# Attention feeding a gelu MLP on one core: a weight tile with its half index moved, and a new order of all steps

## The chip, the core and the metric

The kernel runs on one core of a Trainium2 chip. The metric is the device time of one execution in microseconds (us), lower is better. The engines are TensorE (PE, with its weight loads PEld), VectorE (DVE), ScalarE (ACT), GpSimd (POOL) and SyncE (SP), which issues the transfers.

## The reference, cut to what matters

Four batches of eight heads, 768 positions, 64 values a head; then an MLP from 512 to 2048 and back over the 3072 tokens.

```python
k_sum = k.reshape(B, H, nb, 32, D).max(axis=3)
v_sum = v.reshape(B, H, nb, 32, D).mean(axis=3)
scores_l = where(abs(i - j) < 16, scale * q @ k.T, -1e9)
scores_s = scale * q @ k_sum.T + log(32)
a = softmax(concatenate([scores_l, scores_s]))
x = (a @ concatenate([v, v_sum]))           # to (tokens, 512)
out = gelu(x @ w_in) @ w_out                # exact gelu
```

## The kernel before

All products run in 16-bit pairs: a value is a high part plus a low part, and a product of two values is three matmuls (high by high, high by low, low by high). The first six of 24 attention units use 32-bit matmuls instead.

**Attention.** Unit u is one batch, four heads and 256 query rows. Its steps are `scores` (PE, into the tile pss), `add_mask` or `evac` (out of pss to s), `maximum` (one all-partition reduction on POOL, line 858), `shift` (DVE, line 863) and `exponent` (ACT, line 866), the split into 16-bit parts `s_p_hi` (ACT) and `p_lo` (DVE), `sums` and `values` (PE, into psn and psv), then `norm_take`, `norm_cross`, `norm_rec`, `norm_spread`, `norm_mult` (DVE and ACT, which read psn and psv and free them), and `x_hi`, `x_lo`, the split of the result into the tile xos. The 32-bit units have `f_scores`, `f_sums` and `f_values` in place of the PE steps.

**First MLP product.** Chunk c is 256 tokens (units 2c and 2c+1). For chunks 0 to 3, `phase1 c i` multiplies the chunk by the i-th block of 256 columns of w_in. The remaining tokens are four groups b = 2 to 5 of two chunks; a group's product with w_in is done with seven block products in place of eight: `sp b q n` is product n of 1 to 7 for quarter q of the hidden columns, 12 matmuls each (line 1059). Products 1, 6, 7 and 4 of a quarter add up, one after the other, in one bank y; products 2 and 5 open the banks x and z, and 3 adds to z. Between them `snap b q n` (ACT, line 1070) copies the running sum y to SBUF after products 1, 6 and 7, `comb` (DVE, line 1077) adds such a copy to x or z, and `s_gelu`, `sg_hi`, `sg_lo` make the two parts of the second product's input in the tile gg. The banks y, x and z of all quarters share three places (the tag psh).

**Where the copies go.** The 16-bit w_in weights are in the tile ww: part z (high, low), row block k, column block i, and a half e of 128 columns within the block. Half e = 1 of the first two row blocks is read by no product once chunks 0 to 3 are done, and `snap` writes its copies there:

```python
z = (3 * q + n - 1) % 4
snaps[b, q, n] = ww[:, z // 2, z % 2, :, 1, :].bitcast(F32)
```

Product 1 reads half e = 0 of the same two row blocks as weights.

**Second MLP product.** `phase2 c i` is 12 matmuls of 128x512 (lines 1107 to 1109) into the tile pso; `store` (ACT, line 1114) and `put` (SP) carry it out. There is one pso bank, so the next one waits for `store`. Groups 4 and 5 use seven products here too (`so`, line 1295).

**Weights.** w_in and w_out come as 64-bit values; `wi_bits i 0..2` and `wo_bits` (DVE, lines 456, 461, 465) take the 32-bit value out of the raw bits, `wi_hi` (ACT) and `wi_lo` (DVE) split it into ww.

**What sets the order.** Everything is one list, ORDER, of 1778 steps. Each engine works through its instructions in the order of that list; waits between engines are placed by the framework wherever two instructions touch the same memory. A table SLOTS says which of a tag's buffers each tile takes. `fill` steps are matmuls on ones in the first 37 us, whose result nobody reads.

Of the kernel before, what the change touches and what calls it, by code (L numbers as in the profile page):

```python
# [88 lines left out]
fetch_k 1 3, f_sums 2, evac 3, load_q 4, norm_mult 1, s_k_hi 4, x_hi 1, norm_take 2, wi_hi 5, fill 10, k_lo 4, fetch_k
1 0, x_lo 1, f_mask 4, wi_bits 1 0, f_values 2, maximum 3, load_k 5, s_q_hi 4, load_v 3, load_vs 3, phase1 0 4, wi_lo  # L90
5, shift 3, exponent 3, norm_cross 2, wi_hi 3, wi_bits 1 1, q_lo 4, load_v 4, wi_bits 1 2, fetch_w_in 6 2, phase1 0 0,
gelu 0 0, norm_rec 2, load_vs 4, phase1 0 5, norm_spread 2, f_sums 3, wi_lo 3, norm_mult 2, prep_k 1 3, wi_hi 1,
s_k_hi 5, norm_take 3, k_lo 5, scores 4, f_values 3, gelu 0 4, x_hi 2, wi_lo 1, phase1 0 3, phase1 0 1, norm_cross 3,
x_lo 2, load_q 5, wi_bits 6 0, wi_hi 2, evac 4, norm_rec 3, wi_lo 2, gelu 0 5, norm_spread 3, fetch_w_in 7 3, phase1 0
2, g_hi 0 5, g_hi 0 0, s_q_hi 5, prep_k 1 0, fetch_w_out 0 4, norm_mult 3, g_lo 0 0, x_hi 3, gelu 0 1, gelu 0 3, g_lo
0 5, maximum 4, x_lo 3, gelu 0 2, phase1 1 5, phase1 1 4, shift 4, g_hi 0 1, q_lo 5, wi_bits 7 0, g_hi 0 4, fetch_k 1
1, wo_bits 0 0, exponent 4, g_hi 0 2, fetch_w_out 1 5, g_lo 0 1, g_hi 0 3, wi_bits 6 1, wo_bits 0 1, g_lo 0 3, wo_bits
0 2, load_mask, wo_hi 0, g_lo 0 4, wi_bits 6 2, f_sums 4, f_values 4, f_mask 5, scores 5, phase1 1 2, wi_bits 7 1,
# [5 lines left out]
6, fetch_w_out 4 4, wo_bits 3 1, norm_spread 4, wo_hi 2, phase1 1 6, s_k_hi 6, g_lo 0 2, gelu 1 0, phase1 1 7, wo_bits
3 2, fetch_w_out 5 5, shift 5, exponent 5, k_sums 1 0, k_lo 6, wo_hi 3, norm_mult 4, g_hi 1 0, load_q 7, phase2 0 1,
wo_lo 2, wo_bits 4 0, wo_lo 3, x_hi 4, wo_bits 4 1, f_sums 5, wo_bits 5 0, g_hi 0 6, load_vs 5, wo_bits 4 2, f_mask 6,
wo_bits 5 1, norm_take 5, load_k 7, wo_bits 5 2, scores 6, phase2 0 2, s_q_hi 7, f_values 5, evac 6, fetch_w_out 6 4,
wo_hi 4, wo_lo 4, g_hi 0 7, wo_hi 5, wo_lo 5, norm_cross 5, norm_rec 5, norm_spread 5, fetch_v 1 2, x_lo 4, f_mask 7,
# [5 lines left out]
7, wo_bits 7 2, fetch_v 1 0, wo_lo 6, fetch_v 1 3, sums 6, wo_hi 7, s_k_hi 9, fetch_v 2 1, phase1 2 7, wo_lo 7,
norm_take 6, phase2 0 6, prep_v 1 0, k_lo 9, phase2 0 7, store 0 0, fetch_k 2 3, prep_v 1 3, evac 7, maximum 7, prep_v
2 1, phase2 1 0, phase2 1 2, phase2 1 4, norm_cross 6, g_hi 2 6, prep_k 2 3, load_k 8, wt_add 1 0, s_q_hi 9, shift 7,
q_lo 9, g_hi 2 1, g_lo 2 1, load_vs 6, v_hi 6, g_lo 2 0, gelu 2 3, load_vs 7, wt_add 1 1, v_lo 6, s_k_hi 8, fetch_v 2
2, put 0 0, load_q 8, fetch_k 2 0, k_lo 8, load_k 11, g_lo 2 4, gelu 2 7, phase2 1 6, g_lo 2 6, norm_rec 6, values 6,
v_hi 7, load_v 8, exponent 7, v_lo 7, norm_spread 6, scores 9, phase1 2 2, prep_k 2 0, load_v 9, g_hi 2 3, s_q_hi 8,
s_k_hi 11, wt_add 1 2, s_p_hi 7, q_lo 8, add_mask 9, phase1 2 5, store 1 0, load_q 11, k_lo 11, p_lo 7, norm_mult 6,  # L120
maximum 9, x_hi 6, values 7, sums 7, load_vs 8, prep_v 2 2, x_lo 6, s_q_hi 11, wt_hi 1, q_lo 11, scores 8, g_hi 2 7,
wt_lo 1, norm_take 7, load_vs 9, shift 9, norm_cross 7, norm_rec 7, phase2 1 1, phase2 1 3, phase2 1 5, load_q 10,
add_mask 8, put 1 0, maximum 8, load_k 10, gelu 2 2, norm_spread 7, norm_mult 7, v_hi 9, x_hi 7, x_lo 7, v_hi 8, store
# [1326 lines left out]
```

## Time and profile before

| | |
|---|---|
| median of 3 runs | 569.73 us (568.25 to 572.7) |
| the profiled execution | 572.59 us, of which the span from first to last instruction is 570.8 us |
| TensorE busy | 556.9 us, 98% of the span |
| VectorE busy | 477.3 us, 84% |
| ScalarE busy | 382.0 us, 67% |
| GpSimd busy | 90.4 us, 16% |
| mean granted TensorE clock | 0.991 of full speed |

The profiled execution is 2.9 us above the median of the three runs. Busy shares of PE count a matmul from its start to its modelled end, and matmuls overlap, so a busy PE may still have short gaps between starts; a row with idle time before it is a true wait.

### The profile page before, as it was taken

The page shows a single profiled execution, that of the slowest core. Times are in us where ns is not written, and L with a number is a line of the kernel's source. Part 1 is how long each engine was busy: PE and PEld are TensorE (multiplying, and loading weights), DVE is VectorE, ACT ScalarE, POOL GpSimd, SP SyncE. Part 2 cuts the span into 40 slices and gives each one's busy share as a digit, 9 for nine tenths or more (in the row PEclk, how much of TensorE's full clock was granted, in tenths as well). Part 3 has the DMA queues.
Part 4 walks back from the last instruction along what each step waited for, and adds up shares of the span by engine and source line. Part 5 has one row for each costly group of instructions (what it writes and reads, how often), then busy time and mean ns, then how long its engine had stood idle before and what let it go on. Part 6 is the DMA issues. An engine that isn't in the chain of part 4 may idle for free.

```text
span 570.8 us, 13982 instructions
## 1 busy us (share of the span) xinstructions
PE 556.9 (98%) x6011; PEld 404.4 (71%) x6011; DVE 477.3 (84%) x660; ACT 382.0 (67%) x663; POOL 90.4 (16%) x42
## 2 busy tenths in 40 slices
PE   8969999999999999999979999999999999999997
PEld 4548887584766766667745677766567788888886
DVE  5999999999989899987995777788689999638831
ACT  3758775866696996878962769887547565545621
POOL 3532221202222250031222030203000000000000
PEclk9999999999999999999979999999999999999999
DMA  8969465656644433345251313220000000000101
GB/s 328 396 239 335 154 258 189 206 160 188 199 123 120 140 98 96 84 135 154 74 162 61 87 46 96 76 64 20 20 20 1 20 1 1 11 1 1 65 10 65
DMA packets 29230, 64.30 MB, mean 113 GB/s; under 512 B 2800, under 2 KB 8688, under 8 KB 29168
## 3 DMA queue, kind: packets, MB, share of 16 engines
q1 hardware_dynamic: 29168, 63.41, 33.8%
q8 instruction: 47, 0.77, 0.5%
...
HBM read 55.34 MB, written 6.29 MB: 108 GB/s over the span
## 4 chain that ended last, share of the span: by engine, by line
PE 79%; DVE 14%; ACT 3%; DMA 1%; issue 1%; POOL 1%; SPq 0%; DVEq 0%; POOLq 0%
PE psy L1059 14%; PE pso L1107 9%; PE pso L1109 9%; PE pso L1108 9%; PE psz L1059 7%; PE psd_y L1295 4%; PE psx L1059 4%; PE pso_y L1295 3%; PE psh L988 3%; PE pss_x L1295 3%; PE psh L989 3%; PE psh L990 3%; PE psv L911 3%; PE pss L829 3%; PE psv_z L1295 2%; DVE wt L465 2%
## 5 line engine op out<-in xcount | busy, mean ns | idle before, releaser
L858 POOL PARTITION_ALL_REDUCE m<-s x23 | 79.9, 3472 | 295.7 <-DVE s L849 94.7
L1107 PE MATMUL pso<-w_out_h,gg 128*128 128x512 f16 x256 | 97.2, 380 | 0.0
L1108 PE MATMUL pso<-w_out_l,gg 128*128 128x512 f16 x256 | 97.1, 379 | 0.0
L1109 PE MATMUL pso<-w_out_h,gg 128*128 128x512 f16 x256 | 97.1, 379 | 0.0
L1059 PEld LDWEIGHTS <-wt 128*128 128x128 f16 x768 | 74.9, 98 | 11.9 <-issue 0.4
L988 PE MATMUL psh<-xos,ww 128*128 128x256 f16 x256 | 70.3, 275 | 0.1
L989 PE MATMUL psh<-xos,ww 128*128 128x256 f16 x256 | 70.2, 274 | 0.2 <-DVE xos L968 0.2
L990 PE MATMUL psh<-xos,ww 128*128 128x256 f16 x256 | 70.1, 274 | 0.0
L1059 PE MATMUL psy<-xos,wt 128*128 128x256 f16 x576 | 70.0, 273 | 0.0
L1059 PEld LDWEIGHTS <-ww 128*128 128x128 f16 x576 | 56.4, 99 | 13.7 <-ACT ww L1070 3.7
L1109 PEld LDWEIGHTS <-gg 128*128 128x128 f16 x256 | 25.0, 98 | 30.4 <-issue 0.3
L1107 PEld LDWEIGHTS <-gg 128*128 128x128 f16 x256 | 25.0, 98 | 26.4
L1108 PEld LDWEIGHTS <-gg 128*128 128x128 f16 x256 | 25.1, 98 | 26.1
L1295 PEld LDWEIGHTS <-gg 128*128 128x128 f16 x384 | 37.5, 98 | 4.7 <-DVE gg L1187 0.3
L1070 ACT ACTIVATE ww<-psy 128x512 f32<-128x512 f32 x48 | 28.0, 589 | 16.2 <-PE psy L1059 15.3
L1091 DVE SCALAR_TENSOR_TENSOR gg<-g,gg 128x512 f16<-128x512 f32 x32 | 24.1, 764 | 8.7 <-ACT gg L1087 8.5
L863 DVE TENSOR_TENSOR s<-s,m 128x1024 f32<-128x1024 f32 x21 | 25.5, 1214 | 3.4 <-POOL m L858 3.4
L988 PEld LDWEIGHTS <-ww 128*128 128x128 f16 x256 | 25.1, 98 | 4.0 <-issue 0.2
L1059 PE MATMUL psy<-xos,ww 128*128 128x256 f16 x192 | 24.8, 282 | 3.2 <-ACT ww L1070 3.2
L1187 DVE SCALAR_TENSOR_TENSOR gg<-h,gg 128x512 f16<-128x512 f32 x32 | 21.6, 685 | 7.5 <-ACT gg L1184 7.3
L989 PEld LDWEIGHTS <-ww 128*128 128x128 f16 x256 | 25.2, 98 | 3.7 <-issue 0.3
L990 PEld LDWEIGHTS <-ww 128*128 128x128 f16 x256 | 25.2, 98 | 3.4 <-issue 0.4
...
## 6 DMA issues: line engine op xcount, KB each, us to landing
...
```

The source lines that it names most:

```text
L858: nc.gpsimd.partition_all_reduce(out_ap=self.m32, in_ap=self.s32, channels=P, reduce_op=bass_isa.ReduceOp.max)
L863: nc.vector.tensor_tensor(out=self.s32, in0=self.s32, in1=self.m32, op=ALU.subtract)
L988: nc.tensor.matmul(ph[:, e, :], wh, xh, start=(k == 0), stop=False)
L989: nc.tensor.matmul(ph[:, e, :], wh, xl, start=False, stop=False)
L990: nc.tensor.matmul(ph[:, e, :], wl, xh, start=False, stop=(k == NCC - 1))
L1059: nc.tensor.matmul(ps[:, e, :], ws, xx, start=(first and e == 0 and k == 0 and m == 0), stop=(k == 1 and m == 2), skip_group_check=True,)
L1070: nc.scalar.activation(snaps[b, q, n], split8(acc[b, q, "y"]), AF.Copy)
L1091: nc.vector.scalar_tensor_tensor(out=g_part(o // 2, q, 1, fs), in0=g32t.pop((b, q, o)), scalar=SC_G, in1=g_part(o // 2, q, 0, fs), op0=ALU ...
L1107: nc.tensor.matmul(p, gh, w_out_h[:, f, :], start=(f == 0), stop=False)
L1108: nc.tensor.matmul(p, gh, w_out_l[:, f, :], start=False, stop=False)
L1109: nc.tensor.matmul(p, gl, w_out_h[:, f, :], start=False, stop=(f == NFC - 1))
L1295: nc.tensor.matmul(ps, g, ww_, start=(first and e == 0 and k == 0), stop=(e == 1 and k == 2), skip_group_check=True,)
```

## The change

The tile ww gets its half index e ahead of the column block i, so that each half of a row block is one contiguous piece; all lines that read or write ww follow. The steps of ORDER are the same 1778, none added or left out, in a new order, and SLOTS is new to fit. Of both tables only a line is shown.

```diff
 ORDER = '''
-fill 1, load_q 0, fetch_k 0 0, load_m16, f_mask 0, prep_k 0 0, k_pack 0, f_scores 0, prep_k_end 0 0, fetch_w_in 0 0,
+load_q 0, fill 1, fetch_k 0 0, prep_k 0 0, load_m16, prep_k_end 0 0, k_pack 0, fetch_w_in 0 0, k_sums 0 0, load_ind,
...
     "ks16": (
-        "01101010"
+        "01010101"
     ),
...
-    ww = const.tile([P, 2, NCC, NFC // 2, 2, P], F16, name="ww")
+    ww = const.tile([P, 2, NCC, 2, NFC // 2, P], F16, name="ww")
...
     def w_part(i, z, ks=slice(0, NCC)):
-        return ww[:, z, ks, i].rearrange("p k e j -> p k (e j)")
+        return ww[:, z, ks, :, i].rearrange("p k e j -> p (k e) j")
...
     def wi_rows(i):
-        return wt[:, i].rearrange("p (k n) -> p k n", k=NCC)
+        return wt[:, i].rearrange("p (r j) -> p r j", j=P)
...
-                wh, wl = (ww[:, z, k, i, e, :] for z in range(2))
+                wh, wl = (ww[:, z, k, e, i, :] for z in range(2))
...
-                    wh, wl = (ww[:, z, 2 * w[0] + k, i, w[1], :] for z in range(2))
+                    wh, wl = (ww[:, z, 2 * w[0] + k, w[1], i, :] for z in range(2))
...
     def snap(b, q, n):
         z = (3 * q + n - 1) % 4
-        snaps[b, q, n] = ww[:, z // 2, z % 2, :, 1, :].bitcast(F32)
+        snaps[b, q, n] = ww[:, z // 2, z % 2, 1].bitcast(F32)
```

ORDER is two lines longer, so every line number behind it is two higher in the changed kernel.

The first place is TensorE in the middle of the kernel, where before the last matmuls of `phase2 4 6` (pso_4_0) are followed by `sp 3 1 1` (psy_3_1), on PE before:

```order
L1108 LDWEIGHTS gg_92
L1108 MATMUL pso_4_0_4201<-w_out_l_91,gg_92 128x512
L1109 LDWEIGHTS gg_92
L1109 MATMUL pso_4_0_4201<-w_out_h_90,gg_92 128x512
L1059 LDWEIGHTS ww_86 [waits Activation_49]
L1059 MATMUL psy_3_1_4471<-xos_89,ww_86 128x256 [waits PE_49]
```

In the change `scores 18`, `sums 16`, `values 16`, `phase2 5 0` and `sp 3 1 2` (psx_3_1) stand between the two, and the weight load of `sp 3 1 1` has no wait; on PE now, the last matmuls of `sp 3 1 2` and the first of `sp 3 1 1`:

```order
L1061 LDWEIGHTS ww_86
L1061 MATMUL psx_3_1_4640<-xos_89,ww_86 128x256
...
L1061 LDWEIGHTS ww_86
L1061 MATMUL psy_3_1_4653<-xos_89,ww_86 128x256 [waits DVE_49]
L1061 LDWEIGHTS ww_86
L1061 MATMUL psy_3_1_4653<-xos_89,ww_86 128x256
```

The wait on ScalarE is gone from the weight load; the matmul behind it waits for a VectorE step, the one that frees its bank.

ScalarE at the same place before, from `store 4 0` (ot_4_0) by `s_q_hi 20`, `s_gelu 2 3 2` and two `sg_hi` to `snap 3 0 1` (ww<-psy_3_0):

```order
L1114 ACTIVATE ot_4_0_4456<-pso_4_0_4201 128x512 [waits DMAHW0_49,PE_49]
L794 ACTIVATE qh_20_4458<-q32_20_4298 128x512 [waits DMAHW1_49]
L1084 ACTIVATE g32_2_3_2_4461<-psy_2_3_3944 128x512 [waits DVE_49]
L1087 ACTIVATE gg_92<-g32_2_2_3_4153 128x2x256
L1087 ACTIVATE gg_92<-g32_2_3_2_4461 128x2x256 [waits Activation_49]
L1070 ACTIVATE ww_86<-psy_3_0_4395 128x8x64
```

And ScalarE now:

```order
L1086 ACTIVATE g32_2_2_2_4532<-psy_2_2_3667 128x512 [waits DVE_49]
L1089 ACTIVATE gg_92<-g32_2_2_2_4532 128x2x256 [waits Activation_49]
L1116 ACTIVATE ot_4_0_4536<-pso_4_0_4135 128x512 [waits DMAHW4_49,PE_49]
L1029 ACTIVATE xos_89<-x32s_88 128x512 [waits DVE_49]
L1072 ACTIVATE ww_86<-psy_3_0_4399 128x512
```

Three instructions fewer stand between `store 4 0` and `snap 3 0 1`.

The second place is ScalarE some 10 us earlier, around `snap 2 3 3` (ww<-psy_2_3), which PE needs before `sp 2 3 4`, and `s_gelu 2 3 2` (g32<-psy_2_3), which frees the bank that `sp 3 0 1` takes in the change. Before:

```order
L965 ACTIVATE xos_89<-x32s_88 128x512
L1070 ACTIVATE ww_86<-psy_2_3_3944 128x8x64 [waits PE_49]
L1087 ACTIVATE gg_92<-g32_2_2_1_4232 128x2x256 [waits Activation_49]
L602 ACTIVATE k_all_93<-ks16_3_0_4352 128x2x4x24 [waits DVE_49] x2
L942 ACTIVATE rc_15_4389<-dent_15_4241 128x16
```

And now, with `exponent 16` (s32_16) and its table load ahead, `s_k_hi 18` (k_all), `norm_cross 15` (rc_15) and a table load in between:

```order
L868 ACT_TABLE_LOAD
L868 ACTIVATE s32_16_4181<-s32_16_4181 128x1024 [waits DVE_49]
L1072 ACTIVATE ww_86<-psy_2_3_3945 128x512 [waits PE_49]
L1089 ACTIVATE gg_92<-g32_2_2_1_4184 128x2x256 [waits Activation_49]
L739 ACTIVATE k_all_93<-k32_18_4029 128x10x64 [waits DMAHW1_49]
L944 ACTIVATE rc_15_4370<-dent_15_4361 128x16 [waits DVE_49]
L949 ACTIVATE rc_15_4370<-dent_15_4361 32x8 [waits Activation_49]
L949 ACTIVATE rc_15_4370<-dent_15_4361 32x8 x3
L1086 ACT_TABLE_LOAD [waits DVE_49]
L1086 ACTIVATE g32_2_3_2_4377<-psy_2_3_3945 128x512 [waits PE_49]
```

`exponent 16` moved ahead of `snap 2 3 3`; `s_gelu 2 3 2` moved up from behind `store 4 0`. Over the whole kernel ScalarE has 36 table loads in place of 34.

VectorE at the same place, from `add_mask 16` (s32_16<-pss_16) to `shift 16`, on which `exponent 16` waits, before:

```order
L849 SCALAR_TENSOR_TENSOR s32_16_4230<-mask_sb_79,pss_16_3977 128x1024
L1077 TENSOR_TENSOR g32_2_2_1_4232<-psz_2_2_4128,ww_86 128x512 [waits DVE_49,PE_49]
L934 STREAM_TRANSPOSE dent_15_4241<-psn_15_4219 128x256 [waits PE_49]
L589 TENSOR_REDUCE ks32_3_4228<-kp_3_0_4167 128x24 [waits DMAHW5_49]
L803 TENSOR_TENSOR ql_18_4296<-q32_18_4120,qh_18_4169 128x512 [waits DMAHW2_49]
L597 CAST ks16_3_0_4352<-ks32_3_4228 128x48 [waits DVE_49]
L598 TENSOR_TENSOR ks16_3_0_4352<-ks32_3_4228,ks16_3_0_4352 128x48 [waits DVE_49]
L1091 SCALAR_TENSOR_TENSOR gg_92<-g32_2_2_2_4118,gg_92 128x2x256
L1091 SCALAR_TENSOR_TENSOR gg_92<-g32_2_2_1_4232,gg_92 128x2x256 [waits Activation_49]
L863 TENSOR_TENSOR s32_16_4230<-s32_16_4230,m32_16_4244 128x1024 [waits Pool_49]
```

And VectorE now:

```order
L851 SCALAR_TENSOR_TENSOR s32_16_4181<-mask_sb_79,pss_16_3977 128x1024
L963 TENSOR_TENSOR x32s_88<-psv_14_4033,dent_14_4094 128x512 [waits DVE_49]
L1079 TENSOR_TENSOR g32_2_2_1_4184<-psz_2_2_4099,ww_86 128x512 [waits PE_49]
L640 TENSOR_REDUCE vs_3_3646<-vb_3_2_3908 96x32 [waits DMAHW6_49]
L1093 SCALAR_TENSOR_TENSOR gg_92<-g32_2_2_0_3897,gg_92 128x2x256 [waits Activation_49]
L970 TENSOR_TENSOR xos_89<-x32s_88,xos_89 128x512
L865 TENSOR_TENSOR s32_16_4181<-s32_16_4181,m32_16_4312 128x1024 [waits Pool_49]
```

`norm_take 15` (dent_15), `q_lo 18` (ql_18) and two `sg_lo` (gg) stand behind `shift 16` now; `norm_mult 14` and an `x_lo` (xos) stand between the two steps.

The third place is VectorE near the start, from `norm_mult 0` (x32s<-psv_0) to `norm_mult 1` (x32s<-psv_1), before:

```order
L961 TENSOR_TENSOR x32s_88<-psv_0_316,dent_0_285 128x512 [waits PE_49]
L465 SCALAR_TENSOR_TENSOR wt_87<-gg_92,wt_87 128x1024 [waits DVE_49]
L968 TENSOR_TENSOR xos_89<-x32s_88,xos_89 128x512 [waits Activation_49]
L934 STREAM_TRANSPOSE dent_1_390<-psn_1_348 128x256 [waits PE_49]
L456 TENSOR_SCALAR wt_87<-gg_92 128x1024 [waits DMAHW1_49]
L461 SCALAR_TENSOR_TENSOR wt_87<-gg_92,wt_87 128x1024 [waits DVE_49]
L950 RECIPROCAL rc_1_393<-rc_1_393 128x16 [waits Activation_49]
L954 STREAM_TRANSPOSE dent_1_390<-rc_1_393 128x512 [waits DVE_49]
L465 SCALAR_TENSOR_TENSOR wt_87<-gg_92,wt_87 128x1024
L961 TENSOR_TENSOR x32s_88<-psv_1_363,dent_1_390 128x512 [waits DVE_49,PE_49]
```

And now:

```order
L963 TENSOR_TENSOR x32s_88<-psv_0_314,dent_0_282 128x512 [waits PE_49]
L467 SCALAR_TENSOR_TENSOR wt_87<-gg_92,wt_87 128x1024 [waits DVE_49]
L936 STREAM_TRANSPOSE dent_1_368<-psn_1_356 128x256 [waits DVE_49,PE_49]
L970 TENSOR_TENSOR xos_89<-x32s_88,xos_89 128x512 [waits Activation_49]
L458 TENSOR_SCALAR wt_87<-gg_92 128x1024 [waits DMAHW1_49]
L463 SCALAR_TENSOR_TENSOR wt_87<-gg_92,wt_87 128x1024 [waits DVE_49]
L952 RECIPROCAL rc_1_395<-rc_1_395 128x16 [waits Activation_49]
L956 STREAM_TRANSPOSE dent_1_368<-rc_1_395 128x512 [waits DVE_49]
L467 SCALAR_TENSOR_TENSOR wt_87<-gg_92,wt_87 128x1024
L963 TENSOR_TENSOR x32s_88<-psv_1_372,dent_1_368 128x512 [waits DVE_49,PE_49]
```

`norm_take 1` (the transpose of psn_1) moved ahead of `x_lo 0`; the rest stands as it did. TensorE's own steps up to `f_values 2` stand in the same order in both.

## Rows read from the trace of the kernel before

**Rows 1.** The page, part 1: busy time, share of the span, instructions.

```profile
PE 556.9 (98%) x6011; PEld 404.4 (71%) x6011; DVE 477.3 (84%) x660; ACT 382.0 (67%) x663; POOL 90.4 (16%) x42
```

**Rows 2.** Windows: length, busy time (instructions) of each engine, granted clock, DMA.

```profile
40.00:60.00 20.00, 18.76 (x245) 16.16 (x246) 19.53 (x28) 15.37 (x29) 7.25 (x4) 0.91 0.82 290
60.00:280.00 220.00, 219.61 (x2632) 153.82 (x2630) 208.16 (x278) 171.08 (x281) 41.89 (x14) 1.00 0.47 147
280.00:300.00 20.00, 16.78 (x160) 10.50 (x160) 19.74 (x28) 14.53 (x28) 4.39 (x2) 0.85 0.47 148
...
294.90:297.60 2.70, 2.70 (x16) 1.67 (x20) 2.63 (x6) 0.40 (x1) 0.00 (x0) 0.50 0.95 282
297.60:300.40 2.80, 2.80 (x92) 2.33 (x94) 2.80 (x5) 2.78 (x5) 0.00 (x0) 0.50 0.31 101
```

**Rows 3.** Waits of PE: who for whom, total, times, longest.

```profile
PE psy L1059 <- ACT ww L1070: 3.2, 1, 3.2
PE psv L775 <- POOL m L858: 3.2, 1, 3.2
```

**Rows 4.** The chain that ended last, 276 to 301 us: start, us, what.

```profile
285.13 1.31 PE psz L1059 x12
...
291.66 0.60 ACT ot L1114
...
294.84 2.74 PE psy L1059 x12
```

**Rows 5.** Timeline of DVE, 276 to 292 us: start, us, instruction.

```profile
278.31 0.44 DVE L934 STREAM_TRANSPOSE dent<-psn 128x256 f32<-128x256 f32 x1
...
279.50 0.88 DVE L803 TENSOR_TENSOR ql<-q,qh 128x512 f16<-128x512 f32 x1
...
281.37 1.29 DVE L1091 SCALAR_TENSOR_TENSOR gg<-g,gg 128x512 f16<-128x512 f32 x2
282.57 1.22 DVE L863 TENSOR_TENSOR s<-s,m 128x1024 f32<-128x1024 f32 x1
...
286.57 0.68 DVE L1077 TENSOR_TENSOR g<-psz,ww 128x512 f32<-128x512 f32 x1
```

**Rows 6.** Timelines of DVE, PE, ACT and POOL in turn, 33 to 41 us.

```profile
33.29 1.52 DVE L968 TENSOR_TENSOR xos<-x32s,xos 128x512 f16<-128x512 f32 x1
34.73 0.44 DVE L934 STREAM_TRANSPOSE dent<-psn 128x256 f32<-128x256 f32 x1
...
37.84 2.70 DVE L465 SCALAR_TENSOR_TENSOR wt<-gg,wt 128x1024 int32<-128x1024 int32 x1
40.46 0.68 DVE L961 TENSOR_TENSOR x32s<-psv,dent 128x512 f32<-128x512 f32 x1
...
35.07 0.19 PE L829 MATMUL pss<-qh,k_all 64*128 64x64 f16 x2
...
36.38 1.02 ACT L845 ACTIVATE s<-pss 128x1024 f32<-128x1024 f32 x1
...
37.57 3.22 POOL L858 PARTITION_ALL_REDUCE m<-s  x1 [3.30 <-ACT s L845]
```

**Rows 7.** Groups of DVE by form: busy us, mean ns.

```profile
L465 DVE SCALAR_TENSOR_TENSOR wst<-x32s,wst 128x1024 int32<-128x1024 int32 x4 | 4.8, 1209 | 0.0
```

**Rows 8.** Timeline of ACT, 276 to 291 us.

```profile
278.42 0.63 ACT L1084 ACTIVATE g<-g 128x512 f32<-128x512 f32 x1
...
279.48 0.58 ACT L1070 ACTIVATE ww<-psy 128x512 f32<-128x512 f32 x1
...
281.76 0.21 ACT L942 ACTIVATE rc<-dent 128x16 f32<-128x16 f32 x1
282.01 0.89 ACT L947 ACTIVATE rc<-dent 32x8 f32<-32x8 f32 x4
282.91 1.28 ACT L866 ACT_TABLE_LOAD   x1
284.20 1.06 ACT L866 ACTIVATE s<-s 128x1024 f32<-128x1024 f32 x1
```

More of the change, by code (lines that the diff above doesn't have):

```diff
@@ L89 @@
[L89 to L98, printed above, removed]
@@ L104 @@
[L104 to L108, printed above, removed]
@@ L114 @@
[L114 to L123, printed above, removed]
@@ new lines @@
+2 0 1, s_gelu 2 1 1, sg_hi 2 1 1, maximum 14, sg_lo 2 0 1, sp 2 2 2, shift 15, comb 2 2 0, shift 14, norm_cross 13,
+s_q_hi 16, fetch_v 3 2, q_lo 16, exponent 14, sg_hi 2 1 2, s_p_hi 14, sp 2 3 2, phase2 3 7, norm_rec 13, load_q 18,
+exponent 15, sp 2 3 1, snap 2 3 1, sg_lo 2 1 3, norm_spread 13, k_lo 16, sg_lo 2 1 1, fetch_k 3 0, sp 2 2 7, scores
+16, p_lo 14, norm_mult 13, load_k 18, comb 2 3 0, values 14, sums 14, store 3 1, sg_lo 2 1 2, norm_take 14, s_p_hi 15,
+x_hi 12, sp 2 2 5, norm_cross 14, prep_k 3 0, snap 2 2 3, prep_k_end 3 0, sp 2 3 6, phase2 4 0, snap 2 3 2, p_lo 15,
@@ new lines @@
+x_hi 13, s_gelu 2 2 0, comb 2 2 3, sp 2 2 3, norm_rec 14, norm_spread 14, sp 2 2 4, add_mask 16, norm_mult 14, comb 2
+2 1, s_gelu 2 2 3, sp 2 3 5, values 15, s_gelu 2 3 0, scores 17, sg_hi 2 2 0, sums 15, load_v 16, sg_hi 2 3 0, maximum
+16, sp 2 3 7, prep_v 3 2, phase2 4 2, sg_lo 2 2 0, s_gelu 2 2 1, fetch_k 3 2, x_lo 13, put 3 1, shift 16, exponent 16,
+snap 2 3 3, sg_hi 2 2 1, sp 2 3 4, norm_take 15, sg_lo 2 3 0, fetch_k 3 3, comb 2 3 3, prep_k 3 2, s_k_hi 18,
+norm_cross 15, x_lo 12, s_gelu 2 3 2, sp 2 3 3, sg_hi 2 2 3, s_p_hi 16, sg_lo 2 2 1, s_gelu 2 3 3, load_vs 16, k_lo
@@ new lines @@
+3 1 7, norm_mult 16, phase2 4 1, s_k_hi 20, q_lo 19, scores 19, add_mask 19, s_gelu 3 0 0, s_gelu 3 0 2, values 17,
+v_lo 18, sums 17, norm_take 17, norm_cross 17, norm_rec 17, put 5 0, maximum 19, sp 3 0 3, phase2 4 3, phase2 4 5,
+s_gelu 3 0 3, sg_hi 3 0 0, sg_lo 3 0 0, k_lo 20, shift 19, load_k 21, phase2 4 7, norm_spread 17, s_p_hi 18, comb 3 0
+1, s_gelu 3 0 1, sg_hi 3 0 1, exponent 19, sp 3 2 1, p_lo 18, sp 3 1 5, s_k_hi 21, snap 3 2 1, snap 3 1 3, store 4 1,
+sums 18, norm_mult 17, load_q 21, values 18, s_q_hi 21, scores 20, k_lo 21, norm_take 18, sp 3 2 6, phase2 5 1,
@@ new lines @@
+shift 20, load_vs 20, v_hi 20, values 19, comb 3 2 3, sums 19, sp 3 2 4, s_q_hi 22, q_lo 22, sg_lo 3 0 2, x_hi 16,
+norm_take 19, sp 3 2 3, comb 3 2 1, add_mask 21, snap 3 3 1, sp 3 3 6, norm_cross 19, phase2 5 5, maximum 21, sg_hi 3
+1 2, snap 3 3 2, s_gelu 3 2 1, sg_lo 3 1 2, phase2 5 7, exponent 20, s_gelu 3 2 2, sp 3 3 7, put 4 1, norm_rec 19, sp
+3 3 2, norm_spread 19, sg_lo 3 2 0, shift 21, v_lo 20, sg_hi 3 2 2, load_k 23, sp 3 3 5, store 5 1, s_p_hi 20,
+norm_mult 19, sg_lo 3 2 2, snap 3 3 3, sp 3 3 4, comb 3 3 0, load_vs 22, x_hi 19, phase2 6 0, comb 3 3 3, s_gelu 3 3
```

319 lines of the change are left out of this document (163 added, 156 removed).

## The prediction

> **What bounds the kernel now.** The page's first part comes first: TensorE is busy 98% of the span, VectorE 84%, ScalarE 67% [rows 1]. A reader should see that nothing is left to gain but TensorE's few pauses, and that VectorE is the only other engine near its limit. The windows say where the pauses are: from 60 to 280 us TensorE is busy 219.61 us of 220 at a granted clock of 1.00, with VectorE busy 208.16 of the 220; from 40 to 60 us and from 280 to 300 us the clock is 0.91 and 0.85 [rows 2]. The waits of TensorE then give two of 3.2 us each and no other of that size: `sp 3 1 1` (psy, L1059) for ScalarE's write into ww (`snap`), and `f_values 2` (psv, L775) for a line on GpSimd [rows 3]. Both happen just before or in the windows with the low clock.
>
> The chain of waits shows the first closely. `phase2 4 6` ends and releases `store 4 0` on ScalarE at 291.66; the chain goes on through ScalarE's queue, and `sp 3 1 1` starts at 294.84 [rows 4]. Its 12 matmuls take 2.74 us, while 12 of the same shape took 1.31 us at 285.13 [rows 4]. From 294.9 to 300.4 us the granted clock is 0.50, the 1.2 GHz level [rows 2]: 2.70 and 2.80 us, 5.5 us in all, at half speed. The full level, 2.4 GHz, was granted in the 220 us ahead, in which TensorE had hardly paused; it fell after the pause.
>
> Is that wait a true one? What `sp 3 1 1` writes to, a bank that `comb 2 3 1` was the last to read, was free at 286.57 + 0.68 = 287.25 [rows 5], long before 291.6. What it waits for is `snap 3 0 1`, which writes half e = 1 of ww, while `sp 3 1 1` reads half e = 0. The bytes differ; only the interleaved pieces overlap.
>
> **The change part by part.** The sum is made against the profiled execution, 572.59 us (span 570.8, 1.8 around it). The steps are the same, so TensorE's own work stays, and each term is a pause or a stretch of low clock.
>
> *The wait at 291.6.* With e ahead of i the two halves are separate pieces, and in the new order the weight load of `sp 3 1 1` has no wait for ScalarE. The 3.2 us go [rows 3], and with them the stretch at 0.50: 5.5 us at half speed do the work of 2.75, so 2.75 are lost. 3.2 + 2.75 = 6.0 us. The lower bound is 3.2, if the clock falls there for another reason; the upper one 6.0. I take −6.0, since the clock was 1.00 for the 220 us without a pause. What is late next is `comb 3 0 0`, which the matmul of `sp 3 1 1` now waits for on VectorE. ScalarE's `snap 3 0 1` has three instructions fewer ahead of it, so `comb` can start earlier than it could.
>
> *The start.* `f_values 2` waits for `norm_mult 1` (starts 40.46), behind `wi_bits 3 2` (37.84, 2.70 us) [rows 6]. The same operation on 128x1024 elsewhere takes 1.21 us [rows 7]; this one ran beside GpSimd's `maximum 3` (37.57 to 40.79), which started when `evac 3` (L845, 36.38) was done [rows 6]. The first 34 VectorE instructions are the same set in another order, so their sum gains nothing by itself. But `norm_take 1` (0.44 us at 34.73) no longer stands behind `x_lo 0` (1.52 us at 33.29) [rows 6], which lets `norm_cross 1` on ScalarE and `evac 3` behind it go earlier. `evac 3` needs pss, whose last matmul ended at 35.07 + 0.19 = 35.26; so it can be 36.38 − 35.26 = 1.1 us earlier, GpSimd ends 1.1 earlier, and VectorE is let go 1.1 earlier. The bounds are 0, and 5.0 if the wait goes with its clock: 3.2 and 0.09 x 20 = 1.8 [rows 2, 3]. I take −1.1, the value that a chain of rows gives.
>
> Here the trace can be held against a rule. VectorE's instruction with two SBUF inputs took 2.70 us beside GpSimd's reduction, and 1.21 us elsewhere. The Trainium skill, page "SBUF — State Buffer", section "Who interferes with whom", says that such an instruction and a GpSimd instruction that reads SBUF exclude each other, and whichever issues second waits until the first ends. The trace agrees in that `wi_bits 3 2` ended at 40.54, 0.25 us ahead of `maximum 3`'s end. By the rule an earlier `maximum 3` would first wait for the two-input instruction ahead of `wi_bits 3 2`; an estimate from the page is that some half of the gain goes, and the sum would be half a microsecond higher.
>
> *New tight places in the middle.* Before `sp 3 0 1` the changed order needs a bank freed by `s_gelu 2 3 2`, and ScalarE has ahead of that `exponent 16`, `snap 2 3 3`, an `sg_hi`, `s_k_hi 18`, `norm_cross 15` and a table load. From the start of `snap`, by the rows: 0.58 (the snap), 0.63 (`sg_hi`, priced as the `s_gelu` of the same size), 0.79 (`s_k_hi`, an estimate of mine: 640 columns at the rate of 0.63 for 512), 0.21 + 0.89 (`norm_cross`), 1.28 (the table load) and 0.63 (`s_gelu`), in all 5.0 us [rows 8]. TensorE has 12 matmuls of `phase2` and two `sp` between the end of `sp 2 3 7` and `sp 3 0 1`: half of that is two times 1.31 [rows 4], the other half 2.6 (12 matmuls of 128x512 are twice one of 128x256), in all 5.2. So some 0.2 us are spare if `snap` starts at once, and `exponent 16` (1.06 [rows 8]) must not hold it. `exponent 16` waits for `shift 16`. That ended at 282.57 + 1.22 = 283.79 before [rows 5]. Now `norm_take 15` (0.44), `q_lo 18` (0.88) and two `sg_lo` (1.29) stand behind it [rows 5], and what replaces them evens out, so it ends some 2.6 us earlier, at 281.2; `exponent 16` ends at 282.3, and `s_gelu 2 3 2` at 287.3. `sp 3 0 1` is due at the position where the trace has the psz product at 285.13 [rows 4]. The wait would be 2.2 us if VectorE carries its backlog as before, none if it works off 2.2 us more of it, and 5.8 at the worst, had `shift 16` not moved: 283.79 + 1.06 + 5.0 = 289.85, less 285.13 is 4.7, and 1.1 more if TensorE comes earlier by the start's gain. I take +1.5, two thirds of the way to the unchanged backlog, for this place and the one behind `comb 3 0 0` together; a wait of this size is not charged for the clock.
>
> *Costed at nothing.* Two more table loads of 1.28 us on ScalarE, which is 67% busy [rows 1, 8]; one that stood on TensorE's path would cost the 1.28, and the one that does is in the 5.0. Here a rule speaks against the change. The table load at 282.91 ends, and the next instruction starts at 284.20 [rows 8]. The Trainium skill, page "ScalarE: Activation LUTs", section "What ACT_TABLE_LOAD costs", adds a drain of about 1.38 us to each load; the trace shows no gap there, so no drain behind it, but by the page the chain ahead of `sp 3 0 1` would be that much longer, and the sum an estimated 1.4 us higher. The row forms of `snap`, `comb` and the split of w_in move as many elements as before; a tenth more on 16 copies would lie under TensorE's 219.61 of 220 [rows 2]. SP's transfers come in another order, but its bytes are the same; a transfer that is late by 1 us costs up to that in the first 40 us, which the start's bounds hold. The tail keeps its last product, copy and store.
>
> The sum: 572.59 − 6.0 − 1.1 + 1.5 = **567.0 us**, 0.5% below the median. The profiled execution is 2.9 us above the median; if a run at the median has the wait but not all of the rest, it would give 569.73 − 3.2 = 566.5, which leaves the number where it is. 1% (5.7 us) is about what a measurement of this kernel can tell from no change, so the forecast counts as the same.
>
> **The rivals.**
>
> *Slower: the wait moves to `sp 3 0 1`.* VectorE is busy 208.16 of 220 us [rows 2], so it has no room to work off a backlog. For it speaks that 95%, and that ScalarE's chain has 0.2 us to spare; against it, that `shift 16` has less ahead of it. It decides once `exponent 16` ends after 285.13 − 5.0 = 280.1, `shift 16` after 279.1. At its full price, a wait of 5.8 us and 2.75 for the clock that falls behind it: 572.59 − 6.0 − 1.1 + 5.8 + 2.75 = 574.0 us. With one hold of VectorE by GpSimd in the stretch (2.70 − 1.21 = 1.5 us [rows 6, 7]), 575.5, slower than the median by 1%. At a wait of 3.2 it is 571.4.
>
> *Faster: the pause at the start no longer drops the clock.* `f_values 2` waits 2.1 us in place of 3.2, and if the clock then stays, the 1.8 go too: 567.0 − 1.8 = 565.2. If no new wait comes up in the middle either, 563.7, faster by 1.1%. For it: TensorE's steps are the same there, and the wait shrinks. Against it: the shorter wait is still a pause, and the first 40 us have others.
>
> *The layout does nothing.* Another releaser, the bank, or a copy that `comb 3 0 0` needs, ends the wait at the same time. Then only the start gains: 572.59 − 1.1 = 571.5. Against it the bank was free at 287.25 [rows 5], and the new order puts more steps of TensorE between `phase2 4 6` and `sp 3 1 1`.
>
> *By the page on table loads*, 568.4: the trace's row at 284.20 speaks against it.
>
> **How the numbers follow.** The forecast, 565 to 569, has 0.5; the moved wait 0.2 (half of it above 575.4 with what else may go wrong in 1778 moved steps); the faster case 0.2; no effect of the layout 0.07; the drain 0.03. The range reaches from 562.0, the faster case with the middle of the two unknown starts (563.7, and 1.7 more if the start's wait itself shrinks further within its bound of 5.0), to 573.0, which takes in the moved wait at half its price and the layout without effect. Faster by over 1% means below 564.0: 0.20, all of the faster case. Slower by over 1% means above 575.4: 0.10. The rest, 0.70, is within 1%.
>
> **What the profile after would show.** For the first term: no wait of psy for ww among TensorE's waits, and a granted clock of 1.00 from 280 to 300 us. For the second: `maximum 3` starting near 36.5 instead of 37.57, and `wi_bits 3 2` still near 2.7 us. For the third: a wait of a psy product for ScalarE's g (`s_gelu 2 3 2`) near 285 us, of 0 to 2 us; over 3 us the slower rival is right. The layout rival shows as a wait of psy for VectorE's g at the same place. Wrong altogether would be the forecast if new waits appear in the 220 us that had none, or if the first 40 us shift by several us with the transfers' new order.

## The result, and the profile after

The changed kernel takes **561.88 us**, median of five runs (561.66 to 562.35), against 572.54 for five runs of the kernel before (568.25 to 573.01). The ratio is 0.9836, with a 95% interval of 0.9802 to 0.987: 1.6% faster, where 0.5% was forecast. Two things in the times already say more than the median: the changed kernel's runs lie within 0.7 us of each other, those of the kernel before within 4.8. Two executions further on, one of the layout alone at 2614.93 us and one with a step moved at 580.49 us and a clock of 0.947, are far slower than the others of their kernels and are left out of medians and ranges.

The first part of the changed kernel's page, and its row of windows for the three stretches of [rows 2] (columns as there):

```profile
PE 552.6 (99%) x6011; PEld 402.3 (72%) x6011; DVE 472.6 (84%) x660; ACT 385.0 (69%) x665; POOL 94.8 (17%) x42
```

```profile
40.00:60.00 20.00, 20.00 (x248) 17.20 (x246) 19.96 (x27) 17.47 (x25) 6.64 (x3) 1.00 0.93 343
60.00:280.00 220.00, 218.44 (x2615) 152.70 (x2615) 210.31 (x284) 168.77 (x280) 44.24 (x13) 1.00 0.46 145
280.00:300.00 20.00, 20.00 (x215) 12.21 (x213) 18.66 (x28) 16.37 (x27) 3.22 (x1) 1.00 0.39 111
```

Both stretches with a low clock are gone: 1.00 in each, and TensorE is busy for all 20 us of the first and the last. The 220 us between are slightly less full than before, 218.44 against 219.61 [rows 2]. The waits of TensorE (total, times, longest) say where that went:

```profile
PE psn L785 <- ACT s L868: 1.0, 1, 1.0
PE pso_fill_s L409 <- POOL warm L421: 0.9, 1, 0.9
PE psh L991 <- DVE xos L970: 0.8, 2, 0.5
PE psv L777 <- issue: 0.7, 1, 0.7
```

Of the two waits of [rows 3], that of `sp 3 1 1` is gone, and 0.7 us are left of that of `f_values 2` (psv, L777). New is one of 1.0 us, `f_sums 5` for `exponent 5` at 92.7 us, in the middle of a stretch that had no wait before.

Step by step, from the starts of TensorE's steps in the two traces, the span fell by 570.8 − 560.2 = 10.6 us. `phase1 0 4`, the step behind `f_values 2`, starts at 37.98 in place of 43.11: 5.1. The wait ahead of `sp 3 1 1` and the four steps behind it at half clock give 5.95. The steps around `scores 6`, with the wait of `f_sums 5` behind it, take 1.1 back. Small differences make up the other 0.6, among them `phase1 0 4`, whose first matmuls still ran at half clock before.

**The start.** Before, `f_values 2` on TensorE waited 3.19 us and then ran at the low clock:

```profile
41.24 1.94 PE L775 MATMUL psv<-wt,v 128*64 128x64 f32 x32 [3.19 <-POOL m L858]
```

In the changed kernel its matmuls start at 36.89 and take 1.15. These are rows of VectorE in the changed kernel, from 15 to 37 us, and under them those of GpSimd; the instructions ran in nearly the same order as before.

```profile
15.13 0.37 DVE L599 CAST ks<-ks_f 128x48 f16<-128x48 f32 x1
...
19.52 0.70 DVE L458 TENSOR_SCALAR wt<-x32s 128x1024 int32<-128x1024 int32 x1
20.49 2.60 DVE L463 SCALAR_TENSOR_TENSOR wt<-x32s,wt 128x1024 int32<-128x1024 int32 x1
23.13 1.22 DVE L467 SCALAR_TENSOR_TENSOR wt<-x32s,wt 128x1024 int32<-128x1024 int32 x1
...
25.18 2.00 DVE L496 SCALAR_TENSOR_TENSOR ww<-wt,ww 128x1024 f16<-128x1024 f32 x1
...
31.66 0.65 DVE L970 TENSOR_TENSOR xos<-x32s,xos 128x512 f16<-128x512 f32 x1
...
35.01 1.18 DVE L467 SCALAR_TENSOR_TENSOR wt<-gg,wt 128x1024 int32<-128x1024 int32 x1
36.11 0.68 DVE L963 TENSOR_TENSOR x32s<-psv,dent 128x512 f32<-128x512 f32 x1
...
20.12 3.23 POOL L860 PARTITION_ALL_REDUCE m<-s  x1 [4.67 <-ACT s L847]
23.25 4.19 POOL L860 PARTITION_ALL_REDUCE m<-wt  x1
33.01 2.06 POOL L697 COPY v<-w_out_h 24x1024 f32<-24x1024 f32 x1 [5.57 <-DMA v<-in_vw_dram]
35.16 4.12 POOL L860 PARTITION_ALL_REDUCE m<-s  x1
```

`norm_mult 1` (L963) starts at 36.11, 4.35 us ahead of its 40.46 [rows 6]. `wi_bits 3 2` (L467) takes 1.18 in place of 2.70: it was issued at 35.01, 0.15 us ahead of the reduction, and this time the reduction is the longer one, 4.12 in place of 3.22. `x_lo 0` (L970) takes 0.65 in place of 1.52. The kernel before had three more long rows ahead of these, which the prediction doesn't use; under them stand GpSimd's instructions of the time:

```profile
13.89 1.43 DVE L597 CAST ks<-ks_f 128x48 f16<-128x48 f32 x1
...
20.47 2.38 DVE L456 TENSOR_SCALAR wt<-x32s 128x1024 int32<-128x1024 int32 x1
...
24.36 2.80 DVE L465 SCALAR_TENSOR_TENSOR wt<-x32s,wt 128x1024 int32<-128x1024 int32 x1
...
11.09 4.19 POOL L858 PARTITION_ALL_REDUCE m<-s  x1 [9.11 <-ACT s L845]
20.16 3.95 POOL L858 PARTITION_ALL_REDUCE m<-s  x1 [4.88 <-ACT s L845]
24.02 3.39 POOL L858 PARTITION_ALL_REDUCE m<-wt  x1
32.90 1.36 POOL L695 COPY v<-w_out_h 24x1024 f32<-24x1024 f32 x1 [5.50 <-ACT xos L965]
```

Each began while a reduction ran; `x_lo 0` (33.29, 1.52 [rows 6]) began while GpSimd's copy ran. Against the usual 0.19, 0.69 and 1.22 of the same forms, and with 0.87 for `x_lo 0` and 1.49 for `wi_bits 3 2`, VectorE lost 1.24 + 1.69 + 1.58 + 0.87 + 1.49 = 6.9 us up to 41 us. In the changed kernel it lost 0.18 (15.13), 1.38 (20.49) and 0.78 (25.18), in all 2.3. The difference, 4.5, is close to the 4.35 by which `norm_mult 1` came earlier.

**The middle.** ScalarE in the changed kernel, from `exponent 16` to the `s_gelu 2 3 2` that frees the bank for `sp 3 0 1`, and the two products on the chain:

```profile
273.41 1.06 ACT L868 ACTIVATE s<-s 128x1024 f32<-128x1024 f32 x1 [0.65 <-DVE s L865]
275.28 0.60 ACT L1072 ACTIVATE ww<-psy 128x512 f32<-128x512 f32 x1 [0.81 <-PE psy L1061]
...
278.08 1.28 ACT L1086 ACT_TABLE_LOAD   x1
279.37 0.60 ACT L1086 ACTIVATE g<-psy 128x512 f32<-128x512 f32 x1
```

```profile
280.46 1.31 PE psy L1061 x12
294.28 1.31 PE psy L1061 x12
```

`s_gelu 2 3 2` ends at 279.97, and `sp 3 0 1`, which starts at 280.29 in the timeline (the chain counts it from 280.46), has no wait; `sp 3 1 1` (294.28) runs at full speed, 1.31 against 2.74 [rows 4]. On VectorE, `add_mask 16` before, and under it `add_mask 16` and `shift 16` in the changed kernel:

```profile
276.58 1.21 DVE L849 SCALAR_TENSOR_TENSOR s<-mask_sb,pss 128x1024 f32<-128x1024 f32 x1
```

```profile
267.34 1.18 DVE L851 SCALAR_TENSOR_TENSOR s<-mask_sb,pss 128x1024 f32<-128x1024 f32 x1
...
272.17 1.21 DVE L865 TENSOR_TENSOR s<-s,m 128x1024 f32<-128x1024 f32 x1
```

### The profile page after: what moved, and what is told of

The parts are those of the page before. It is cut to its first block, busy times and chain, and to the rows that moved or that the text cites. A ratio compares the mean times of both kernels' runs of the same rounds, so it can differ in the third digit from the quotient of the medians.

```text
span 560.2 us, 13994 instructions
## 1 busy us (share of the span) xinstructions
PE 552.6 (99%) x6011; PEld 402.3 (72%) x6011; DVE 472.6 (84%) x660; ACT 385.0 (69%) x665; POOL 94.8 (17%) x42
## 4 chain that ended last, share of the span: by engine, by line
PE 75%; DVE 21%; issue 2%; DMA 1%; ACT 1%; SPq 0%; DVEq 0%
PE psy L1061 13%; PE pso L1109 9%; PE pso L1110 9%; PE pso L1111 9%; PE psz L1061 7%; PE psd_y L1297 4%; PE pss_x L1297 3%; PE pso_y L1297 3%; PE psx L1061 3%; PE psv L913 3%; PE psh L990 2%; PE psh L991 2%; PE psh L992 2%; PE pss L831 2%; DVE wt L463 2%
## 5 line engine op out<-in xcount | busy, mean ns | idle before, releaser
L860 POOL PARTITION_ALL_REDUCE m<-s x23 | 82.6, 3593 | 284.1 <-DVE s L851 114.2
L1093 DVE SCALAR_TENSOR_TENSOR gg<-g,gg 128x512 f16<-128x512 f32 x32 | 22.7, 711 | 8.0 <-ACT gg L1089 7.9
L999 ACT ACTIVATE g<-psh 128x512 f32<-128x512 f32 x32 | 18.9, 593 | 11.4 <-DVE gg L1008 8.6
```

What stands on the lines that cost most here:

```text
L860: nc.gpsimd.partition_all_reduce(out_ap=self.m32, in_ap=self.s32, channels=P, reduce_op=bass_isa.ReduceOp.max)
L1093: nc.vector.scalar_tensor_tensor(out=g_part(o // 2, q, 1, fs), in0=g32t.pop((b, q, o)), scalar=SC_G, in1=g_part(o // 2, q, 0, fs), op0=ALU ...
```

## The experiments

Two theories stood for the middle: the overlap of the copy with the weights (the layout) and the place of `sp 3 1 1` in the order. Two stood for the start: that VectorE is held beside GpSimd, and that the sequence itself, of transfers or of VectorE's steps, is better. Times are medians, with the range over a kernel's runs; in these comparisons the kernel before took 570.62 to 571.76 us. The 561.88 of the changed kernel is from the result above; no run of it stands beside them.

**The layout alone** (the order of before):

```diff
-    ww = const.tile([P, 2, NCC, NFC // 2, 2, P], F16, name="ww")
+    ww = const.tile([P, 2, NCC, 2, NFC // 2, P], F16, name="ww")
...
```

> The old order with the new layout of ww. If the wait of sp 3 1 1 at 291.6 us is the false overlap of the copy with the weights, it goes with its stretch of low clock: 3.2 + 2.75 = 6.0 us less than before, about 566.5 us, a granted clock of 1.00 from 280 to 300 us, and the first 60 us as before (f_values 2 near 41 us). If the order took that wait away and the layout nothing, 571 to 573 us and the wait stays, with another releaser.

564.54 us, three executions (562.99 to 565.9), ratio 0.9893 (0.9853 to 0.9934). The wait at 291 us and the low clock behind it are gone, `phase2 4 6` to `sp 3 1 1` takes 3.4 us less, and `f_values 2` still waits, 2.5 us in the profile. So the layout is enough to remove that wait. The time is 2.0 us below the expected 566.5; in the profiled run the wait of `f_values 2` was shorter than before (2.5 for 3.2) and no clock fell behind it.

**The order alone** (the layout of before):

```diff
-    ww = const.tile([P, 2, NCC, 2, NFC // 2, P], F16, name="ww")
+    ww = const.tile([P, 2, NCC, NFC // 2, 2, P], F16, name="ww")
...
```

> The new order with the old layout of ww. TensorE then waits for ScalarE's copy at three weight loads again (sp 3 1 1, sp 3 3 1, sp 4 2 1). In the trace of the changed kernel those copies end at 291.6, 339.8 and 416.54, and the products start at 294.0, 342.5 and 416.56; so if place in the order decides, the layout is not needed here: 561.9 us, the same as the changed kernel within 0.5. If the layout is what gives the middle its gain, 565 to 568 us with a wait of 3 us or more at one of the three.

562.73 us (562.56 to 562.91), ratio 0.9864 (0.983 to 0.9897). No wait for a copy is among TensorE's. For this wait the order is enough too: the two parts of the change remove the same wait, and either would do. The time is 0.85 us above the changed kernel's, where at most 0.5 was expected; what that difference is stays open.

**One step moved** in the kernel before, the copy ahead of the store on ScalarE:

```diff
-store 4 0, s_q_hi 20, norm_rec 15, s_gelu 2 3 2, p_lo 16, sg_hi 2 2 3, sg_hi 2 3 2, norm_spread 15, snap 3 0 1,
+snap 3 0 1, store 4 0, s_q_hi 20, norm_rec 15, s_gelu 2 3 2, p_lo 16, sg_hi 2 2 3, sg_hi 2 3 2, norm_spread 15,
```

> The kernel before with one step moved: snap 3 0 1 ahead of store 4 0 on ScalarE; the layout stays, and with it the overlap. If the wait at 291 us is only the copy's late place in ScalarE's queue, it goes as with the new layout: 563 to 566 us, no wait of psy for ww. If the copy has another reason to be late, 570 to 573 us.

566.28 us, six executions (564.79 to 568.86), ratio 0.992 (0.9891 to 0.9949). The wait is gone here as well: the copy itself runs at 288.07, while `phase2 4 6` is still on TensorE. So nothing held the copy but its place in ScalarE's queue. The median lies 1.7 us above the layout's; the two differ in the clock (0.994 to 1.00 in these six, 1.00 in the layout's three; where in a run it fell isn't recorded), and the profiled runs, both at 1.00, are 0.3 us apart (563.0 and 562.7 of span).

**The head of the new order in the old one**: the first 125 steps, up to `phase1 0 4`, in the new order, the rest as before.

```diff
-fill 1, load_q 0, fetch_k 0 0, load_m16, f_mask 0, prep_k 0 0, k_pack 0, f_scores 0, prep_k_end 0 0, fetch_w_in 0 0,
+load_q 0, fill 1, fetch_k 0 0, prep_k 0 0, load_m16, prep_k_end 0 0, k_pack 0, fetch_w_in 0 0, k_sums 0 0, load_ind,
...
```

> The old order and layout, but the first 125 steps (up to phase1 0 4) in the order that the new one has for them. If the start's gain comes from that stretch, f_values 2 starts near 36.8 us in place of 41.1, the clock stays at 1.00 from 40 to 60 us, and 5.1 us go: about 567.4 us, with the wait at the middle (3.2 us) as before. If the gain of the start is given back later, or hangs on what follows, 570 to 573 us.

567.59 us (565.41 to 569.09), ratio 0.9948 (0.992 to 0.9976). `f_values 2` starts at 36.76, as expected. In the profiled run the wait at the middle is there, and the clock behind it isn't low; its waits, and its windows:

```profile
PE psy L1060 <- ACT ww L1071: 3.2, 1, 3.2
```

```profile
40.00:60.00 20.00, 20.00 (x250) 17.48 (x249) 19.95 (x28) 17.26 (x32) 5.57 (x3) 1.00 0.97 360
60.00:280.00 220.00, 219.01 (x2612) 151.93 (x2611) 208.63 (x280) 170.84 (x283) 42.69 (x13) 1.00 0.46 146
280.00:300.00 20.00, 16.78 (x193) 10.05 (x192) 18.84 (x26) 13.18 (x21) 3.22 (x1) 1.00 0.42 133
```

That is new: the same 3.2 us of pause, without the price in clock. Over its nine runs, the granted clock and the time go together but for one (567.32): 1.00 at 565.41, 565.68 and 567.32, 0.996 and 0.997 at 566.63 to 567.61, 0.994 at 567.71 to 569.09. The kernel before does the same in one comparison: 567.29, 567.39 and 567.93 at 1.00, nine of the ten others at 0.994 or below and between 570.11 and 572.83. In these runs a pause costs its own length each time, and the clock only in some executions.

**The changed kernel with the old head**, the counterpart (its first 126 steps in the old order):

> The changed kernel, but its first 126 steps (up to phase1 0 4) in the old order. The counterpart: f_values 2 near 41 us, a low clock behind it, no wait at 291 us; 561.9 + 5.1 = 567.0 us. If the parts don't add up (a late start is absorbed by slack behind it), 562 to 564 us.

566.36 us (565.4 to 567.17), ratio 0.9935 (0.9902 to 0.9967): 4.5 us more than the changed kernel, with the wait of 3.2 us at the start and a clock of 0.91 from 40 to 60 us. Little behind it absorbs the late start (5.1 us were expected). All five runs have a clock of 0.996 or 0.997; the profiled one shows that it fell behind this pause.

**Both local cures in the old order**: the layout and the head, the other 1653 steps as before.

> The old order with the new layout of ww and the first 125 steps in the new order: both local cures, and the other 1653 steps as before. If the two waits are all that the change removes, its runs have no pause and a clock of 1.00, and take 565.4 (the best run with the new head alone) less 3.2 = 562.2 us, within 0.6 of the changed kernel's 561.9, with a spread under 1 us. If the new order of the other steps gives or costs something of its own, 563 us or more, or 561 or less.

562.9 us (562.08 to 566.26), ratio 0.9863 (0.9813 to 0.9914). Three of four runs are within 1.3 us of the changed kernel's median, one is at 566.26 with a clock of 0.997. So most of the gain needs only the two cures. The median is 0.7 us above the expected 562.2 and the spread is 4.2 us where under 1 was expected, so whether the rest of the new order adds up to a microsecond, or steadiness, stays open with four runs.

**Short reductions.** GpSimd's `maximum` of units 0 to 3 takes 64 of 1024 columns, and the shift reads these 64 for all columns; only the first is shown. In the kernel before:

```diff
+            n = TQ if self.u < 4 else UCOLS
...
-                out_ap=self.m32, in_ap=self.s32, channels=P, reduce_op=bass_isa.ReduceOp.max
+                out_ap=self.m32[:, :n], in_ap=self.s32[:, :n], channels=P, reduce_op=bass_isa.ReduceOp.max
...
```

> The kernel before, but the reductions over partitions of units 0 to 3 take 64 of the 1024 columns, and the shift uses these 64 for all columns (left out: the maximum of the other columns). Everything else, the order too, stays. If the late f_values 2 comes from VectorE being held beside GpSimd's reductions, the long rows of VectorE up to 41 us (1.43, 2.38, 2.80, 2.70 us) fall to their usual 0.2, 0.7, 1.2 and 1.2, norm_mult 1 starts near 35 in place of 40.5, f_values 2 near 36.5 us, and 4.5 us or more go from a run: 565 to 567.5 us against 570.7. If the order of transfers or of VectorE's steps sets it, f_values 2 stays within 1 us of 41.1 and the time within 1 us.

566.13 us (565.06 to 567.47), ratio 0.9916 (0.9889 to 0.9943). The old order, and the same instructions of VectorE that were long before:

```profile
14.23 0.19 DVE L597 CAST ks<-ks_f 128x48 f16<-128x48 f32 x1
...
19.59 0.69 DVE L456 TENSOR_SCALAR wt<-x32s 128x1024 int32<-128x1024 int32 x1
...
22.03 1.23 DVE L465 SCALAR_TENSOR_TENSOR wt<-x32s,wt 128x1024 int32<-128x1024 int32 x1
...
27.93 0.70 DVE L456 TENSOR_SCALAR wt<-gg 128x1024 int32<-128x1024 int32 x1 [0.58 <-DMA gg<-in_w_in_dram]
...
35.25 1.18 DVE L465 SCALAR_TENSOR_TENSOR wt<-gg,wt 128x1024 int32<-128x1024 int32 x1
36.36 0.68 DVE L966 TENSOR_TENSOR x32s<-psv,dent 128x512 f32<-128x512 f32 x1
```

Every one is back at its usual duration, `norm_mult 1` starts at 36.36 and `f_values 2` at 37.14. And in the changed kernel:

> The changed kernel with the same four short reductions (the same part left out). Its VectorE was held for 2.35 us up to 36 us, TensorE waited 0.87 us there: by the theory of the holds f_values 2 starts within 1 us of the same kernel with the old order, and the time falls by 0.5 to 1.5, to 560.4 to 561.4 us; the two kernels then differ by the middle alone, 3.2 us and what the clock adds. If the new order's own sequence gives the start, f_values 2 stands some 4 us earlier here than in the old order with short reductions.

561.58 us (561.16 to 561.8), ratio 0.9852 (0.9788 to 0.9915). The time fell by 0.3 us where 0.5 to 1.5 was expected. `f_values 2` starts at 37.27: without the long reductions the old order and the new one reach it within 0.15 us of each other. So the holds are what made `f_values 2` late in the old order, and the new one gains by having fewer of them. Whether the sequence by itself would give more can't be seen here: in both runs VectorE then waits for a transfer of w_in (0.58 us up to 27.93, 1.02 up to 28.07), and so both stand at the same next limit.

**One place on VectorE.** In the changed kernel `wi_bits 3 2` goes behind `norm_mult 1`, so that the reduction is issued first:

```diff
-wi_bits 3 2, fill 10, s_k_hi 4, f_sums 2, norm_mult 1, x_hi 1,
+fill 10, s_k_hi 4, f_sums 2, norm_mult 1, wi_bits 3 2, x_hi 1,
```

> The changed kernel with wi_bits 3 2 behind norm_mult 1 on VectorE: one step moved by one place. In the changed kernel wi_bits 3 2 was issued at 35.01 us, 0.15 us ahead of the reduction, which then took 4.12 us. By the theory of the holds it now comes second: it takes 2.5 us or more in place of 1.18, the reduction 3.3 in place of 4.12, norm_mult 1 and f_values 2 come up to 0.9 us earlier, but x_lo 1 and the first phase1 product wait 1 to 3 us: 563 to 565.5 us, with the clock falling in some of the runs. If holds play no part, 561 to 562 us, since norm_mult 1 is only earlier.

563.6 us (563.28 to 566.51), ratio 0.9889 (0.9859 to 0.992). VectorE and GpSimd there:

```profile
35.69 2.34 DVE L467 SCALAR_TENSOR_TENSOR wt<-gg,wt 128x1024 int32<-128x1024 int32 x1
...
35.05 3.22 POOL L860 PARTITION_ALL_REDUCE m<-s  x1
```

Whichever comes second is the longer: 2.34 and 3.22 here, 1.18 and 4.12 in the changed kernel. `f_values 2` is 0.8 us earlier and the first product behind it waits 1.6 us for `x_lo 1`. One step moved by one place costs 1.7 us.

**The longest wait that is left**, `f_sums 5` for `exponent 5`: in the changed kernel `wo_hi 2` goes behind `exponent 5` on ScalarE.

```diff
-norm_mult 4, wo_hi 3, wo_hi 2, exponent 5,
+norm_mult 4, wo_hi 3, exponent 5, wo_hi 2,
```

> The changed kernel with wo_hi 2 behind exponent 5 on ScalarE. The longest wait of TensorE that is left (f_sums 5 for exponent 5 at 92.7 us, 1.0 us) should fall to 0 to 0.3: 560.9 to 561.2 us. If another releaser stands right behind (wo_lo 2 for phase2 0 2), 561.5 to 562.5.

562.61 us (562.25 to 563.46), ratio 0.9875 (0.9821 to 0.9929): no gain, and 0.1 us above what the second theory gave. The waits of TensorE and GpSimd's rows of that run say why, and one thing more:

```profile
PE psv L777 <- POOL m L860: 2.4, 1, 2.4
PE pso L1110 <- DVE w_out_l L556: 1.0, 1, 1.0
```

```profile
32.86 1.03 POOL L697 COPY v<-w_out_h 24x1024 f32<-24x1024 f32 x1 [5.46 <-DMA v<-in_vw_dram]
34.75 3.31 POOL L860 PARTITION_ALL_REDUCE m<-s  x1 [0.85 <-ACT s L847]
```

The wait moved on to the next weights (`wo_lo 2`, 1.0 us), as the second theory had it. And `f_values 2` waits 2.4 us again, though no step within the first 80 us was moved: in this execution the transfer that releases the copy on GpSimd landed in time for it to start at 32.86 in place of 33.01, ahead of `wi_bits 3 1`, which then took 2.05 us, and the reduction came ahead of `wi_bits 3 2`. In its profiled run the changed kernel wins this race by 0.15 us; which of the other executions here lost it isn't recorded.

**The pause filled.** The kernel with the old layout and the new head, with four steps of matmuls on ones between `phase2 4 6` and `sp 3 1 1`:

```diff
-sp 3 1 1,
+fill 20, fill 21, fill 22, fill 23, sp 3 1 1,
...
```

> The old order with the new head and the old layout, so with the 3.2 us wait at 290 us, and four steps of matmuls on ones (24 matmuls of 256 columns, some 3.1 us) put between phase2 4 6 and sp 3 1 1. The work of the kernel and the wait for the copy stay; TensorE is busy meanwhile. If the pause is what lowers the clock, no run shows a granted clock below 0.999, and all take 565.0 to 565.8 us, where the same kernel without the filling took 565.4 to 569.1. If the clock falls there for another reason, the spread stays, up to 569.

566.04 us (565.68 to 567.43), ratio 0.991 (0.9877 to 0.9942). All four runs have a granted clock of 1.00, where six of nine had less without the filling. The times were expected at 565.0 to 565.8, and three of the four lie above that. From the start of `phase2 4 6` to that of `sp 3 1 1` it is 6.07 us, against 5.97 without the filling, so 0.1 us is the filling's; the rest isn't explained by it. One run, at 567.43, is long for another reason than the clock, which its time alone doesn't show. That the pause makes the clock fall is supported by this.

## Why the prediction was right and wrong

The direction and the two places were right. The size was not: 561.88 is 5 us below the number and 0.1 under the low end of the range, 562.0. Of the three terms, one held and two failed.

1. **The wait at 291 us, −6.0: held.** 5.95 us between the two profiled runs. Two things of its reasoning need correction. The layout was argued as the cure; the order by itself is one as well, as is moving one copy. In the changed kernel `snap 3 0 1` (291.01, 0.58) is done 2.5 us before `sp 3 1 1` starts, so an overlap would have cost nothing there. The rival by which the layout does nothing is out all the same: alone in the old order it removes the wait. And the 2.75 us of the clock are not part of every run: the profiled run of before (572.59, clock 0.991) had the fall in both places, runs at 1.00 (567.3 to 567.9) in neither. So the whole 6.0 came true because the profiled run is one that paid the clock twice. The prediction saw that this run was 2.9 us above the median and left it; the clock would explain that (runs at 0.994 took 568.6 to 573.3), but that of the median run isn't recorded.

2. **The start, −1.1: the step that failed.** It measured −5.1. The sentence at fault is that the first 34 instructions of VectorE are "the same set in another order, so their sum gains nothing by itself". The sum did gain, 4.5 us, since a duration there depends on what GpSimd does at the same time. The rule for it was in the prediction, with one row (2.70 against 1.21) as its evidence, and it was used for that one row; four more rows of the same kind stood between 13 and 34 us of the trace, three beside reductions and one beside the copy. The short reductions show that the holds are what made `f_values 2` late. The signs that the prediction named for this term, `maximum 3` near 36.5 and `wi_bits 3 2` still near 2.7 us, came out at 35.16 and 1.18. The bound of 5.0 was near, but by another sum than its pause and clock: TensorE reached `f_sums 2` 1.7 us earlier, which the bound left out, the wait shrank by 2.5, and `f_values 2` at the full clock gave 0.8. What the prediction took from the page "SBUF — State Buffer" of the Trainium skill, section "Who interferes with whom", that the instruction issued second waits, is what both orders of the pair show (1.18 and 4.12, 2.34 and 3.22). That it waits until the first ends is not: `wi_bits 3 2`, which takes 1.18 by itself, ended at 38.03 as the second, and the reduction at 38.27. The prediction's own row, an end 0.25 us ahead of the reduction's, says the same and was read as agreement. The estimate from the page, half of the gain lost, was wrong, because here the new order let `wi_bits 3 2` be the first.

3. **New tight places, +1.5: not there.** `exponent 16` started at 273.41 and ended 0.8 us ahead of the copy it might have held. The forecast had `shift 16` 2.6 us earlier, from the steps between `add_mask 16` and it; with TensorE's position taken out (4.7 us between the traces at `sp 2 3 4`), it was 5.7 us earlier. Of this 1.2 us come from the steps between the two. The other 4.6 come from `add_mask 16` itself, whose place the forecast left as it was: it started 6.9 us behind the start of `scores 16`, in place of 11.4. The chain itself was as costed: 279.97 − 275.28 = 4.7 us from the copy to the end of `s_gelu`, against 5.0. The new wait that did come, 1.0 us at `f_sums 5`, was in a place that was not looked at. The prediction named new waits in the 220 us as a sign of being wrong altogether; this one cost about 1 us of the 10.6.

Of the rivals, the faster one came nearest in time (563.7), and its condition, no low clock at the start, is met; but the wait shrank to less than its 2.1 us. The slower one named a wait that didn't arise. The drain behind a table load that the page "ScalarE: Activation LUTs" of the Trainium skill states is not seen on this chain: the load at 278.08 takes 1.28 and the next instruction starts at 279.37.

The chances gave 0.20 to faster by over 1%, which is what happened.
